# Reciprocal roots of two neighbouring units in one GpSimd chain, and a rank of its own for every step

## The chip, the cores and the metric

The kernel runs on one core of one Trainium2 chip. The metric is the time on the device in microseconds: 1473.11 us, the median of 3 runs (1471.62 to 1473.71).

## The reference

Agent attention followed by a feed-forward layer with a SoLU and a layer norm, in four batches of 12608 tokens, with 128 channels, 49 agents and 1024 hidden units:

```python
def sm(a, b):                      # softmax over the last axis
    s = scale * (a @ b.transpose(0, 2, 1))
    e = np.exp(s - s.max(-1, keepdims=True))
    return e / (e.sum(-1, keepdims=True) + 1e-09)
agent_v = sm(agents, k) @ v
x = (sm(q, agents) @ agent_v).reshape(B * N, 128)
h = x @ w_in
sm_ = softmax(h)
solu = h * sm_
ln = (solu - mean(solu)) / np.sqrt(var(solu) + 1e-06) * g_ln
out = ln @ w_out
```

q, k and agents are drawn with a standard deviation of 0.8; w_in and w_out arrive as 64-bit floats and are converted on the chip.

## The kernel before, in words

The tokens are worked on in tiles of 128, 99 to a batch, 396 in all. A batch has two stages. In the first (`phase_a`), the keys and values are read in chunks of 1024 (12 and a rest of 320), scored against the agents (line 523), exponentiated, transposed (line 556) and multiplied with the values (line 577); the result, folded with w_in, is a pair of matrices, `mh` and `ml`. The first stage of batch b+1 is run among the tiles of batch b. In the second, `phase_b` forms the softmax of eight tiles of queries against the agents, and then each tile goes through these steps: scores `h` on TensorE (`c_h`, line 867, four matmuls), their maximum on VectorE (`c_max`, line 871), the exponential on ScalarE with its sum S (`c_exp`, line 881), the product u on VectorE (`c_u`, line 886), and the sum of squares Q on ScalarE (`c_sq`, line 892).

Then come the output products. Two tiles are a pair, two pairs are a unit of four tiles. Pairs are of kinds Z and Y in turn (`PAT = "ZYZY"`), so a Z unit and a Y unit are interleaved and end one pair apart; the last four pairs are Z. A Z unit transposes u on TensorE (line 899), evacuates it on ScalarE into `uT` (line 952), splits it on GpSimd into a high and a low part (lines 961 and 965) and multiplies them with the two parts of w_out (`c_w`, line 982); the product stands in a PSUM bank until `c_fin` (line 1053) on VectorE multiplies it by the roots `rB`. A Y unit transposes u in blocks on VectorE (`c_tb`, line 906), moves the blocks with 16 DMAs from SP's queue (`c_mv`, line 916), multiplies in full float (`c_wy`, line 922) and is scaled by its roots `yp` on ScalarE or VectorE (`c_fy`, line 930 or 932).

The roots are formed for each unit once its four tiles' S and Q are there (`c_rstd`): eight instructions on GpSimd over four columns (lines 993 to 1014; the fourth is a power of -1/2, line 1002, then follows one step of Newton's rule), a transposition `yr` on VectorE (line 1018), a DMA `dr` into DRAM (line 1022) and one back: spread over all partitions as `rB` for a Z unit (line 1026), as one column a tile, `yp`, for a Y unit (line 1044). The last unit takes another way, over TensorE.

The order of the work is written out by a planner in the kernel (`Plan`). Each step is an op with engines, a planned cost, a due time, and the ops that it waits for. The planner walks through time; for each engine it looks at the ops that could start within a short margin and takes the one with the smallest due time. The due times are the tile's number plus an offset by kind of step (`DH`, `DMX`, ...), some sixty constants. There are two banks of two for the scores and four single PSUM banks that the planner hands out to all other products. What it writes down is the order of each engine's instructions and of SP's queue; the waits on the chip follow from the data.

Of the kernel before, what the change touches and what calls it, by code (L numbers as in the profile page):

```python
# [16 lines left out]
PSUM = bass.MemoryType.PSUM  # L17

# [7 lines left out]
class Plan:  # L26
# [158 lines left out]
def pair_kinds(n):  # L185

    kinds = ["Z" if i >= n - 4 else PAT[i % len(PAT)] for i in range(n)]
    if kinds.count("Y") % 2:
        kinds[max(i for i in range(n) if kinds[i] == "Y")] = "Z"
# [11 lines left out]
def kernel(  # L201
# [18 lines left out]
    GT = 4  # L220
# [7 lines left out]
    CPR = 514.07  # L228
# [17 lines left out]
    BD0 = 1.55  # L246
    BD1 = 43.9
    BD2 = 323.81
    BD3 = -61.67
    BD4 = 161.19  # L250
    BD5 = -3.79
    DH = -7.09
    DMX = 12.27
    DEX = -557.66
    DU_ = -32.48
    DSQ = 235.38
    DT = -63.56
    DCP = -36.06
    DEV = 13.48
    DLD = -39.18  # L260
    DSP = 47.88
    DW = 22.04
    DR = -5.79
    DF_ = 10.97
    DRB = -20.24
    OUTD = -9.57
    OUTC = -74.75
    VA = 3
    VA1 = 12
    QA = 41.77  # L270
    WA = 314.18
    VLAG = 98.2
    PTB = 4
    SHY = -80.96
    DHR = -337.25
    DHL = -85.23
    DMXR = -12.05
    DMXL = -147.69
    DEXR = 107.68
    DEXL = -205.84  # L280
    DUR = -296.62
    DUL = -37.59
    DSQR = -186.3
    DSQL = -311.69
    DTR = 73.98
    DTL = -151.89
    DEVR = -27.37
    DEVL = -372.85
    DLDR = -297.34
    DLDL = 160.86  # L290
    DSPR = -202.86
    DSPL = -50.83
    DWR = 84.18
    DWL = 1.45
    RBL = -442.9
    ASP = 1.09
    MZ = 2.36
    DTB = -3.22
    DMV = -110.03
    DMS = -223.53  # L300
    MVC = 1
    DWY = 28.21
    DWS = 5.02
    YC = 8
    DFY = 54.59
    DTBR = -12.62
    DTBL = -3.65
    ASTART = -9.62
# [133 lines left out]
    nhalf = const.tile([P, GT], F32, name="nhalf")  # L442
# [35 lines left out]
    def phase_a(b, due, gate):  # L478
# [188 lines left out]
        def kop(c):  # L667
            if c < NC and c not in K:
                old = M1.get(c - 1) if not head else None
                K[c] = op("S", st(kload, c), (0.45, sz(c), 0), -199 + 0.2 * c if head else at(c * 2.55 - 3), gate + [old])  # L670

        def vop(c):
            old = M2.get(c - 1) if not head else M1[3] if 4 <= c < 8 else M1[7] if 8 <= c < NCK else None
            V[c] = op("S", st(vload, c), (0.45, sz(c), 0), -199 + 0.2 * c + VLAG if head else at(c * 2.55 - 2), gate + [old])
# [16 lines left out]
        for c in range(NC):  # L691
# [4 lines left out]
            if not head:  # L696
# [3 lines left out]
            EE[c] = op("A", st(p1_exp, c), 0.665 if c < NCK else 0.742, at(z + 0.5), [N1[c], TT.get(c - EKB)], free=M1[c])  # L700
            TT[c] = op("P", st(p2_t, c), 0.435 * fr(c), at(z + 1), [EE[c], M2.get(c - 2) if not head else None], take=True)
            ET[c] = (op("A", st(p2_et, c, "A"), 0.478 * fr(c), at(z + 1.2), [TT[c]], free=TT[c]) if head and c < HEADA else
                     op(ETE, st(p2_et, c), (0.478 * fr(c), 0.6 * fr(c)), at(z + 1.2), [TT[c]], free=TT[c]))
# [32 lines left out]
    BT, B0, B4, B5, BQ, pT_op, grp_h = {}, {}, {}, {}, {}, {}, {}  # L736
# [17 lines left out]
    def phase_b(k, dues, gate=()):  # L754
# [74 lines left out]
        d1 = op("D", b1, 0.047 + 0.0532 * nt, dues[1], [prev], shy=shy)  # L829
        d2 = op("D", b1s, 0.05 + 0.0532 * nt, dues[1] + 0.1, [d1] + [B4.get((k - 2, q)) for q in range(2)], free=first, shy=shy)  # L830
        a1 = op("A", b2, 0.098 + 0.0402 * nt, dues[2], [d2])
        d3 = op("D", b3, 0.05 + 0.0532 * nt, dues[3], [a1], shy=shy)
        d5 = op("D", b3r, 0.12, dues[3] + 0.2, [d3])
        for q in range(nq):
# [7 lines left out]
            B5[k, q] = op("P", lambda px, q=q: b5(q, px), 0.33 * sc, dues[5] + 2.5 * q, [B4[k, q]], take=True, shy=shy)  # L842
# [9 lines left out]
    order = {"Y": 0, "Z": 0}  # L852
# [20 lines left out]
    def c_exp(x):  # L873
        G, j = slot[x]
        if G not in st:
# [93 lines left out]
    def c_w(i, m0, m1, px=None):  # L969
        G = unit[i]  # L970
        h = units[G][1].index(i)
# [12 lines left out]
    def c_rstd(G):  # L984
        gp = nc.gpsimd
        r = {}

        def r0():
            for z in "txyz":
                r[z] = tiny.tile([P, GT], F32, tag=z, bufs=SB, name=f"{z}{G}")  # L990
            r["yt"] = ycol[G % 2]
            r["yc"] = r["yt"][:, :: SQB // GT]
            gp.tensor_scalar(out=r["t"], in0=st[G]["S"], scalar1=1e-9, scalar2=math.sqrt(1e-6 * DF), op0=ALU.add, op1=ALU.mult)
# [4 lines left out]
        def r2():  # L998
            gp.tensor_tensor(out=r["x"], in0=st[G]["Q"], in1=r["t"], op=ALU.add)

        def r3():
            gp.tensor_tensor(out=r["y"], in0=r["x"], in1=nhalf, op=ALU.pow)
# [13 lines left out]
        def r8():  # L1016
            r["yr"] = tiny.tile([P, SQB], F32, tag="yr", name=f"yr{G}")
# [6 lines left out]
        def sent(e):  # L1024
            rB = st[G]["rB"] = opool.tile([P, GT, GT, SQB], F32, tag="rB", bufs=3, name=f"rB{G}")
            port[e].dma_start(out=rB.rearrange("d a j p -> d (a j p)"),
                              in_=r["dr"].rearrange("j p -> (j p)").unsqueeze(0).to_broadcast([P, P * GT]))

        def d0():
            r["dg"] = epool.tile([P, GT, P], F32, tag="uT", bufs=UTB, name=f"dg{G}")  # L1030
# [7 lines left out]
        def d2():  # L1038
            rB = st[G]["rB"] = opool.tile([P, GT, GT, SQB], F32, tag="rB", bufs=3, name=f"rB{G}")
            nc.scalar.copy(out=rB.rearrange("d a j c -> d j a c"), in_=r.pop("px").rearrange("d (j a c) -> d j a c", a=GT, c=SQB))  # L1040

        def senty(e):
            yp = st[G]["yp"] = tiny.tile([P, GT], F32, tag="yp", name=f"yp{G}")
            port[e].dma_start(out=yp, in_=r["dr"].rearrange("j p -> (j p)").rearrange("(a p) -> p a", p=P))
# [5 lines left out]
    def c_fin(G, j0=0, j1=GT):  # L1050
        rB = obs[G] = st[G]["rB"]
        z = rB.rearrange("d a j c -> d j a c")[:, j0:j1]
# [34 lines left out]
    for q, cost in enumerate((1.23, 0.64, 0.35)):  # L1087
        os_ = op("G", F(sums, q), cost, OUTD, og + [os_])
    om = op("P", mean, 0.22, OUTD, [os_], take=True)
# [9 lines left out]
    TBT, MV, WY, FY, OO, YP, R2, CP = ({} for _ in range(8))  # L1099
    utl, pol = [], {}  # L1100
    nth, seen = {}, {"Y": [], "Z": []}
    for G, (kd, _) in enumerate(units):
        nth[G] = len(seen[kd])
        seen[kd].append(G)
    zpairs = [i for i in range(n // 2) if units[unit[i]][0] == "Z"]
    zix = {i: z for z, i in enumerate(zpairs)}

    def back(G, k):
        z = nth[G] - k
        return seen[units[G][0]][z] if z >= 0 else None  # L1110
    ku = 0
    for x in range(n):
# [3 lines left out]
        isY = kind[x] == "Y"  # L1116
# [9 lines left out]
        MX[x] = op("D", F(c_max, x), 1.13, at(x, DMX, DMXR, DMXL), [H[x, 0], H[x, 1]])  # L1126
# [151 lines left out]
```

## Time and profile before

| | before |
|---|---|
| median of 3 runs | 1473.11 us |
| span of the profiled execution (its own time) | 1472.9 us |
| TensorE matmuls busy | 1444.4 us (98%) |
| TensorE weight loads busy | 1279.7 us (87%) |
| VectorE busy | 1376.2 us (93%) |
| ScalarE busy | 1291.1 us (88%) |
| GpSimd busy | 1071.1 us (73%) |
| DMA | 221.90 MB, mean 151 GB/s |

In the rows below, PE is TensorE's matmuls and PEld its weight loads, DVE VectorE, ACT ScalarE, POOL GpSimd, SP or SPq the queue that issues the DMAs; L12 is line 12 of the kernel. Busy times are of one profiled execution. Matmuls are pipelined and their ends are modelled, so a busy TensorE is not TensorE at its peak. Idle time of an engine that is not the bottleneck costs nothing.

### The profile page before, as it was taken

Reading aid. Unit: us, or ns where it says so; the run is one execution under the profiler, and the core shown is the slowest. Engines: PE = TensorE matmul, PEld = TensorE weight load, DVE = VectorE, ACT = ScalarE, POOL = GpSimd, SP = SyncE. Lnnn points to the kernel's source line nnn. Section 1 sums busy time; section 2 is a strip of 40 time slices with the busy share of each in tenths; the row PEclk is TensorE's granted clock in tenths of the full one; section 3 lists DMA queues with packets and bytes.
Section 4 is the critical chain, followed back from the end, with each engine's and each line's share of the span. In section 5 each row is a group of like instructions: output and inputs, shape, how many; then the busy total and the mean of one; then the engine's idle time right before and its main releaser. Section 6 shows DMA issues by size and latency. Waiting matters only on the chain.

```text
span 1472.9 us, 33358 instructions
## 1 busy us (share of the span) xinstructions
PE 1444.4 (98%) x12033; PEld 1279.7 (87%) x12033; DVE 1376.2 (93%) x2024; ACT 1291.1 (88%) x2486; POOL 1071.1 (73%) x1521
## 2 busy tenths in 40 slices
PE   8889999999999999999999999999999999999998
PEld 4668889898888898899898798998999999999998
DVE  5899999999999999999989899999999999999985
ACT  5489999999898998899987898988989999999985
POOL 2485887777776777688677667787768887887854
PEclk9899999999999999999999999999999999999999
DMA  9356565565456756654746666566455455554541
GB/s 369 130 137 194 145 166 149 152 160 142 130 140 187 183 144 160 155 167 114 191 105 159 175 169 175 142 164 166 113 140 135 116 150 131 132 142 106 138 107 44
DMA packets 113253, 221.90 MB, mean 151 GB/s; under 512 B 47552, under 2 KB 50880, under 8 KB 113088
## 3 DMA queue, kind: packets, MB, share of 16 engines
q1 hardware_dynamic: 113088, 219.77, 55.7%
q8 instruction: 95, 1.56, 0.5%
q14 instruction: 70, 0.57, 0.1%
HBM read 92.87 MB, written 26.15 MB: 81 GB/s over the span
## 4 chain that ended last, share of the span: by engine, by line
PE 64%; DVE 15%; ACT 12%; issue 4%; DMA 3%; SPq 2%; POOL 0%; ACTq 0%; DVEq 0%; POOLq 0%
PE ph L867 16%; PE px L922 16%; PE px L982 13%; PE px L899 8%; DVE u L886 5%; ACT e L881 5%; DVE nm L871 4%; ACT uT L952 3%; ACT e L892 3%; PE px L523 3%; DVE tb L906 3%; PE px L577 3%; PE px L767 2%; SPq L916 2%; PE px L812 1%
## 5 line engine op out<-in xcount | busy, mean ns | idle before, releaser
L881 ACT ACTIVATE e<-ph,nm 128x1024 f32<-128x1024 f32 x396 | 443.3, 1123 | 88.1 <-DVE nm L871 84.4
L871 DVE TENSOR_REDUCE nm<-ph 128x1 f32<-128x1024 f32 x396 | 467.2, 1207 | 31.8 <-PE ph L867 29.9
L886 DVE SCALAR_TENSOR_TENSOR u<-ph,e 128x1024 f32<-128x1024 f32 x396 | 471.7, 1218 | 18.7 <-ACT e L881 15.1
L965 POOL TENSOR_TENSOR uL<-uT,uH 128x1024 fp32r<-128x1024 f32 (+1 forms) x198 | 471.3, 2380 | 12.2
L892 ACT ACTIVATE e<-u,su 128x1024 bf16<-128x1024 f32 x396 | 459.1, 1163 | 20.2 <-DVE u L886 19.6
L922 PE MATMUL px<-w,uY 128*128 128x128 f32 x3072 | 375.6, 276 | 0.0
L922 PEld LDWEIGHTS px<-w,uY 128*128 128x128 f32 x3072 | 359.9, 192 | 13.9 <-issue 8.4
L867 PE MATMUL ph<-mh,pT 128*128 128x512 f32 x792 | 335.4, 423 | 7.7 <-DVE u L886 7.3
L867 PE MATMUL ph<-ml,pT 128*128 128x512 f32 x792 | 312.8, 395 | 1.9 <-DVE ml L653 1.9
L961 POOL TENSOR_SCALAR uH<-uT 128x1024 fp32r<-128x1024 f32 (+1 forms) x198 | 207.8, 1049 | 87.0 <-ACT uT L952 87.0
L982 PE MATMUL px<-uH,wH 128*128 128x256 f32 x816 | 237.8, 291 | 0.4 <-ACT eT L567 0.4
L906 DVE STREAM_TRANSPOSE tb<-u 128x1024 f32<-128x1024 f32 x192 | 235.8, 1233 | 0.7
L982 PE MATMUL px<-uH,wL 128*128 128x256 f32 x816 | 228.4, 280 | 0.0
L982 PE MATMUL px<-uL,wH 128*128 128x256 f32 x816 | 228.0, 279 | 0.0
L952 ACT COPY uT<-px 128x512 f32<-128x512 f32 x394 | 213.7, 597 | 11.7 <-PE px L899 11.1
L899 PE MATMUL px<-ident,u 128*128 128x128 f32 x1632 | 218.1, 275 | 1.1 <-ACT uT L952 0.6
L899 PEld LDWEIGHTS px<-ident,u 128*128 128x128 f32 x1632 | 186.2, 142 | 15.8 <-ACT uT L952 3.8
L867 PEld LDWEIGHTS ph<-mh,pT 128*128 128x128 f32 x792 | 150.1, 190 | 39.5 <-DVE u L886 13.4
L867 PEld LDWEIGHTS ph<-ml,pT 128*128 128x128 f32 x792 | 150.7, 190 | 24.4 <-DVE ml L653 2.3
L982 PEld LDWEIGHTS px<-uH,wH 128*128 128x128 f32 x816 | 153.8, 188 | 15.6 <-issue 11.4
L982 PEld LDWEIGHTS px<-uL,wH 128*128 128x128 f32 x816 | 155.2, 190 | 3.7 <-issue 0.5
L982 PEld LDWEIGHTS px<-uH,wL 128*128 128x128 f32 x816 | 153.7, 188 | 0.0
(127 smaller groups left out, 1570.1 us busy)
## 6 DMA issues: line engine op xcount, KB each, us to landing
uY<-tb SPq DMA_DIRECT2D x768, 128.0 KB, 2.6
qt<-in_qT_dram SPq DMA_DIRECT2D x48, 512.0 KB, 4.2
kt<-in_kT_dram SPq DMA_DIRECT2D x36, 512.0 KB, 4.4
vt<-in_v_dram SPq DMA_DIRECT2D x36, 512.0 KB, 4.1
rB<-dr SPq DMA_DIRECT2D x50, 256.0 KB, 4.1
out_dram<-rB SPq DMA_DIRECT2D x50, 256.0 KB, 2.0
out_dram<-oy SPq DMA_DIRECT2D x48, 256.0 KB, 2.7
kh<-in_kT_dram SPq DMA_DIRECT2D x12, 512.0 KB, 8.7
```

The source lines that it names most:

```text
L867: nc.tensor.matmul(ph[:, sl], lhs, bmats[b]["mh" if m == 0 else "ml"][:, sl], start=(m == 0), stop=(m == 1))
L871: nc.vector.tensor_reduce(out=nms[x], in_=phs[x], op=ALU.max, axis=AX.X, negate=True)
L881: nc.scalar.activation(out=es[x], in_=phs[x], func=AF.Exp, bias=nms.pop(x), accum_out=st[G]["S"][:, j : j + 1])
L886: nc.vector.scalar_tensor_tensor(out=u, in0=phs[x], scalar=INV, in1=es[x], op0=ALU.mult, op1=ALU.mult, accum_out=su)
L892: nc.scalar.activation(out=sq, in_=u, func=AF.Square, bias=su, scale=-float(DF), accum_out=st[G]["Q"][:, j : j + 1])
L899: nc.tensor.transpose(pt[:, kf * P : (kf + 1) * P], us[x][0][:, k0 * P : (k0 + 1) * P], ident)
L906: nc.vector.transpose(to, us[x][0].rearrange("p (k r c) -> p k r c", r=GT, c=SQB))
L922: nc.tensor.matmul(st[G]["po"][:, a * P : (a + 1) * P], yb[G][1][:, a, kf].rearrange("p x c -> p (x c)"), w2[:, kf, :], start=(kf == 0), s ...
L952: nc.scalar.copy(out=rr[x][:, hf * 4 : hf * 4 + 4, :], in_=pt)
L961: nc.gpsimd.tensor_scalar(out=uH, in0=rr[x][:, k0:k1, :], scalar1=1.0, scalar2=0.0, op0=ALU.mult, op1=ALU.add)
L965: nc.gpsimd.tensor_tensor(out=uL, in0=rr[x][:, k0:k1, :], in1=uH.bitcast(F32), op=ALU.subtract)
L982: nc.tensor.matmul(po, wt[:, kf, :], ut[:, kf, :], start=(q == 0), stop=(q == WM - 1))
```

## The change

Neighbouring units, in the order in which they end, share one chain for their roots. `chains` lists them, `link` tells of each unit its chain and its place in it. S and Q are now tiles of eight columns for a chain, of which each unit uses four; the eight GpSimd instructions, the transposition and the DMA `dr` are done once for a chain, after the last tile of its last unit; `rB` and `yp` are read back for each unit as before.

Each op's due time is no longer worked out from the offsets but read from a table in the order in which the ops are made (`RANKS`, a compressed list of 16-bit numbers). The offsets stand in the code with other values, but the table overrides them. Margins of the planner are changed too, and many ops get an `after`, which fixes their order among their like without a wait on the chip. There are other smaller edits: a Y unit's first matmul waits for the scaled output of the Y unit before (`back(G, 1)`, it was `back(G, 2)`), the ring of S and Q holds four chains (it held six units), and there is a third kind of unit, X, with functions of its own, which the pattern does not use.

```diff
+RANKS = (
...
+        raw = zlib.decompress(base64.b85decode(RANKS))
+        self.ranks = [z / 40 - 100 for z in struct.unpack(f"<{len(raw) // 2}H", raw)]
+        self.made = 0
...
     def op(self, eng, fn, cost, due, deps=(), take=False, free=None, after=(), kind=1, shy=0.0):
         o = Op()
+        due = self.ranks[self.made]
+        self.made += 1
...
-    EP = 0.14
-    EA = 0.09
-    ED = 0.0
-    EG = 2.33
-    HLD = -3.7
-    STK = 1.57
+    EP = 0.15
+    EA = 0.1
+    ED = 0.1
+    EG = 1.0
+    HLD = -3.0
+    STK = 1.0
...
-    SB = 6
+    SB = 4
...
+    ends = sorted(range(len(units)), key=lambda G: units[G][1][-1])
+    chains, link = [], {}
+    for z, G in enumerate(ends):
+        if chains and len(chains[-1]) == 1 and units[G][1][-1] - units[chains[-1][0]][1][-1] <= 2 and z < len(ends) - 1:
+            chains[-1].append(G)
+        else:
+            chains.append([G])
+        link[G] = (len(chains) - 1, len(chains[-1]) - 1)
...
+            st["c", c] = [tiny.tile([P, 2 * GT], F32, tag=z, bufs=SB, name=f"{z}{c}") for z in "SQ"]
...
-            st[G] = {
-                "S": tiny.tile([P, GT], F32, tag="S", bufs=SB, name=f"S{G}"),
-                "Q": tiny.tile([P, GT], F32, tag="Q", bufs=SB, name=f"Q{G}"),
-            }
+            st[G] = {z: t[:, u * GT : (u + 1) * GT] for z, t in zip("SQ", st["c", c])}
...
-    def c_rstd(G):
+    def c_rstd(c):
         gp = nc.gpsimd
+        m = len(chains[c]) * GT
+        step = SQB // (2 * GT)
...
-            dr = r["dr"] = dpool.tile([GT * GT, SQB], F32, tag="dr", bufs=4, name=f"dr{G}")
-            port[e].dma_start(out=dr, in_=r["yr"][:: SQB // GT, :])
+            dr = r["dr"] = dpool.tile([GT, 2, GT * SQB], F32, tag="dr", bufs=4, name=f"dr{c}")
+            port[e].dma_start(out=dr.rearrange("a u (j q) -> (a u j) q", q=SQB), in_=r["yr"][::step, :])
...
-        MX[x] = op("D", F(c_max, x), 1.13, at(x, DMX, DMXR, DMXL), [H[x, 0], H[x, 1]])
+        MX[x] = op("D", F(c_max, x), 1.13, at(x, DMX, DMXR, DMXL), [H[x, 0], H[x, 1]], after=[MX.get(x - 1)])
...
-                    prev = op("P", f, 0.224 * YC, x + DWY + DWS * q / (GT * NF // YC), (mv if q == 0 else []) + [prev, FY.get(back(G, 2)) if q == 0 else None] + wready, take=q == 0, kind=4)
+                    prev = op("P", f, 0.224 * YC, x + DWY + DWS * q / (GT * NF // YC), (mv if q == 0 else []) + [prev, FY.get(back(G, 1)) if q == 0 else None] + wready, take=q == 0, kind=4)
...
-        if j == GT - 1:
-            first, rest, turn, send, sent, (d0, d1, d2), senty = c_rstd(G)
-            mine = [2 * z + q for z in units[G][1] for q in range(2)]
+        ci, cu = link[G]
+        if j == GT - 1 and cu == len(chains[ci]) - 1:
+            first, rest, turn, send, sent, (d0, d1, d2), senty = c_rstd(ci)
+            mine = [2 * z + q for z_ in chains[ci] for z in units[z_][1] for q in range(2)]
```

## Rows read from the trace of the kernel before

**Rows 1.** The page's first part: busy us, share of the span, instructions.
```profile
PE 1444.4 (98%) x12033; PEld 1279.7 (87%) x12033; DVE 1376.2 (93%) x2024; ACT 1291.1 (88%) x2486; POOL 1071.1 (73%) x1521
```

**Rows 2.** Busy time by stretch: stretch, length, each engine, granted clock, DMA.
```profile
0.00:120.00 120.00, 102.12 (x835) 70.67 (x836) 98.99 (x177) 77.12 (x162) 61.53 (x92) 0.93 0.64 216
120.00:1200.00 1080.00, 1073.79 (x9010) 959.04 (x9008) 1028.70 (x1502) 971.99 (x1864) 805.18 (x1139) 1.00 0.58 152
1200.00:1400.00 200.00, 199.98 (x1667) 186.31 (x1666) 196.63 (x273) 191.12 (x368) 166.57 (x235) 1.00 0.52 131
1400.00:1473.00 73.00, 68.50 (x528) 63.63 (x526) 51.88 (x75) 50.91 (x96) 37.78 (x57) 1.00 0.27 74
```

**Rows 3.** The same, of line 867 alone: matmuls, then weight loads.
```profile
120.00:1080.00 960.00, 299.01 (x1080) 187.72 (x1080) 1.00 0.59 155
1200.00:1320.00 120.00, 38.73 (x151) 26.35 (x149) 1.00 0.54 136
```

**Rows 4.** Chain that ended last, first batch's keys: start, us, what.
```profile
17.96 1.01 PE px L523 x4
...
26.02 0.44 PE px L556 x4
...
41.44 1.02 PE px L577 x16
```

**Rows 5.** Groups by line: count, busy us, mean ns, idle before.
```profile
L1002 POOL TENSOR_TENSOR y<-x,nhalf 128x4 f32<-128x4 f32 x99 | 100.2, 1012 | 7.7
...
L1014 POOL TENSOR_TENSOR ycol<-y,z 128x4 f32<-128x4 f32 x99 | 20.3, 205 | 8.1
...
L1018 DVE STREAM_TRANSPOSE yr<-ycol 128x32 f32<-128x32 f32 x98 | 19.3, 197 | 4.0 <-POOL ycol L1014 3.8
L993 POOL TENSOR_SCALAR t<-S 128x4 f32<-128x4 f32 x99 | 19.3, 195 | 56.1 <-ACT e L881 51.0
```

**Rows 6.** Timeline of GpSimd, 1196 to 1231 us: start, length, what.
```profile
1197.10 0.19 POOL L993 TENSOR_SCALAR t<-S 128x4 f32<-128x4 f32 x1
...
1206.29 0.19 POOL L993 TENSOR_SCALAR t<-S 128x4 f32<-128x4 f32 x1
...
1209.07 0.20 POOL L1014 TENSOR_TENSOR ycol<-y,z 128x4 f32<-128x4 f32 x1
```

**Rows 7.** Waits of the whole span: us in total, times, longest.
```profile
PEld px L899 <- ACT uT L952: 3.8, 15, 0.8
...
PEld px L812 <- POOL ycol L1014: 1.6, 2, 0.8
```

**Rows 8.** Timeline of SP's queue, 1204 to 1231 us.
```profile
1205.18 0.38 SPq L1026 DMA_DIRECT2D rB<-dr  x1
1207.42 10.59 SPq L916 DMA_DIRECT2D uY<-tb  x16
1218.11 0.54 SPq L1022 DMA_DIRECT2D dr<-yr  x1
```

**Rows 9.** Timeline of VectorE, 1204 to 1231 us.
```profile
1210.02 0.19 DVE L1018 STREAM_TRANSPOSE yr<-ycol 128x32 f32<-128x32 f32 x1
...
1222.43 0.67 DVE L1053 TENSOR_TENSOR rB<-px,rB 128x512 f32<-128x512 f32 x1
```

**Rows 10.** DMA issues: count, KB each, median us to landing.
```profile
rB<-dr SPq DMA_DIRECT2D x50, 256.0 KB, 4.1
...
dr<-yr SPq DMA_DIRECT2D x98, 2.0 KB, 1.8
```

**Rows 11.** Timelines of ScalarE and of TensorE, 1204 to 1231 us.
```profile
1207.10 1.13 ACT L930 ACTIVATE oy<-px,yp 128x128 f32<-128x128 f32 x4
...
1210.25 1.95 PE L922 MATMUL px<-w,uY 128*128 128x128 f32 x16
```

**Rows 12.** Chain that ended last, 0 to 125 us: start, us, what.
```profile
47.98 1.42 DVE ca_out L368
...
54.95 1.60 POOL w L368
...
56.57 1.51 DVE w L368
...
60.39 2.26 DVE nm L871 x2
```

More of the change, by code (lines that the diff above doesn't have):

```diff
@@ L1 @@
+import base64
 import math
+import struct
+import zlib
 from contextlib import ExitStack
@@ L187, in pair_kinds @@
     kinds = ["Z" if i >= n - 4 else PAT[i % len(PAT)] for i in range(n)]
-    if kinds.count("Y") % 2:
-        kinds[max(i for i in range(n) if kinds[i] == "Y")] = "Z"
+    for k in "YX":
+        if kinds.count(k) % 2:
+            kinds[max(i for i in range(n) if kinds[i] == k)] = "Z"
     units, open_ = [], {}
@@ L244 @@
     WC = 12
[L246 to L257, printed above, removed]
[L258 to L267 removed]
+    BD0 = -19.07
+    BD1 = 170.81
+    BD2 = -212.77
+    BD3 = 221.79
+    BD4 = -125.09
+    BD5 = 89.47
+    DH = -1001.84
+    DMX = 537.76
+    DEX = -742.92
+    DU_ = -73.14
+    DSQ = 242.69
+    DT = -560.39
+    DCP = -36.06
+    DEV = -708.6
+    DLD = 138.29
+    DSP = 144.95
+    DW = 41.63
+    DR = -236.61
+    DF_ = 250.94
+    DRB = 136.25
+    OUTD = 224.28
+    OUTC = 373.93
     VA = 3
     VA1 = 12
[L270 to L272 removed]
+    QA = 346.14
+    WA = -635.12
+    VLAG = 213.44
     PTB = 4
     SHY = -80.96
[L275 to L288, printed above, removed]
[L289 to L300 removed]
+    DHR = 270.45
+    DHL = -42.04
+    DMXR = -1193.55
+    DMXL = 333.78
+    DEXR = 361.3
+    DEXL = 36.12
+    DUR = 35.14
+    DUL = -402.67
+    DSQR = 322.29
+    DSQL = 377.68
+    DTR = -72.36
+    DTL = -80.02
+    DEVR = -59.2
+    DEVL = 324.83
+    DLDR = -297.34
+    DLDL = 69.77
+    DSPR = -732.04
+    DSPL = 136.84
+    DWR = -382.0
+    DWL = -6.98
+    RBL = -442.9
+    ASP = 1.072
+    MZ = 1.612
+    DTB = 266.92
+    DMV = 56.0
+    DMS = -370.6
     MVC = 1
[L302 to L303 removed]
+    DWY = -89.82
+    DWS = 936.93
     YC = 8
[L305 to L308, printed above, removed]
+    DFY = -17.85
+    DTBR = -297.4
+    DTBL = -15.69
+    XPOS = 3
+    XGAP = 2
+    DXP = 3.0
+    DXS = 3.0
+    DXW = 6.0
+    DFX = 8.0
+    ASTART = 3.06
     AEND = -155.17
@@ L1098 @@
     H, MX, EX, U, SQ, T, EV, LD, SH, SP, W, FIN, RB, TN = ({} for _ in range(14))
[L1099 to L1110, printed above, removed]
+    TBT, MV, WY, FY, OO, YP, R2, UYD, SD = ({} for _ in range(9))
@@ new lines, with back @@
+    utl, pol, LY, LZ = [], {}, {}, {}
+    sets = ("Y", "Z", "X", "YX", "ZX")
+    nth, seen = {}, {z: [] for z in sets}
+    for G in ends:
+        kd = units[G][0]
+        for z in sets:
+            if kd in z:
+                nth[G, z] = len(seen[z])
+                seen[z].append(G)
+    def back(G, k, z=None):
+        z = z or units[G][0]
+        m = nth[G, z] - k
+        return seen[z][m] if m >= 0 else None
+    gseq = sorted([(2.0 * i, i) for i in range(n // 2) if units[unit[i]][0] == "Z"]
+                  + [(min(2.0 * units[G][1][-1] + 1.5 + XPOS + XGAP * h, n - 4.4 + 0.1 * h), (G, h)) for G in seen["X"] for h in range(2)], key=lambda z: z[0])
@@ new lines, with spare @@
+    gix = {k: z for z, (_, k) in enumerate(gseq)}
+    AL, R0, UA, last_t = {}, {}, [os0], None
+    closed, opened, room = [], [], {}
+    for _, k in gseq:
+        G, h = k if isinstance(k, tuple) else (unit[k], units[unit[k]][1].index(k))
+        if h == 0:
+            assert len(opened) <= 1
+            room[G] = closed[: len(closed) - (1 - len(opened))][-1:]
+            opened.append(G)
+        else:
+            opened.remove(G)
+            closed.append(G)
+    def spare(G):
+        return [FIN.get(z) for z in room[G]]
@@ new lines, in gprev, with split, unit_x @@
+    def gprev(k, m):
+        z = gix[k] - m
+        return gseq[z][1] if z >= 0 else None
+    def split(k, src, d, f, g, k0=0, k1=NF):
+        a = op("G", f, 0.2 + 0.115 * (k1 - k0), d, src + [W.get(gprev(k, ZB))], after=AL.get(gprev(k, 1), []))
+        AL.setdefault(k, []).append(a)
+        return a, op("G", g, 0.2 + 0.268 * (k1 - k0), d + 0.02, [a])
+    late = []
+    def unit_x(pos, k):
+        G, h = k
+        for q in (2 * h, 2 * h + 1):
+            SH[G, q], SP[G, q] = split(k, MV[G][q * GT : q * GT + GT], pos + DXP + DXS * q / GT, F(c_xh, G, q), F(c_xl, G, q))
+        prev = W.get(gprev(k, 1))
+        for m0 in range(0, WM, WC):
+            m1 = min(m0 + WC, WM)
+            lead = m0 == 0 and h == 0
+            f = (lambda px, m1=m1: c_w(k, 0, m1, px)) if lead else F(c_w, k, m0, m1)
+            prev = op("P", f, 0.1172 * (m1 - m0), pos + DXW + 2.0 * m0 / WM,
+                      [SH[G, 2 * h], SP[G, 2 * h], SH[G, 2 * h + 1], SP[G, 2 * h + 1]] + wready + [prev] + (spare(G) if lead else []),
+                      take=lead, kind=3)
+            if lead:
+                pol[G] = [prev]
+        W[k] = prev
+        UYD[G] = UYD.get(G, []) + [SP[G, 2 * h], SP[G, 2 * h + 1]]
+        if h:
+            FIN[G] = op("D", F(c_fin, G), 0.62, pos + DFX, [prev, RB[G]], free=pol[G][-1])
+            OO[G] = op("S", F(c_out, G), (0.48, 0.26, 0), pos + DFX, [FIN[G]])
@@ L1115 @@
         i = x // 2
-        isY = kind[x] == "Y"
+        kd = kind[x]
+        while late and late[0][0] < x:
+            unit_x(*late.pop(0))
         if t % UB == 0:
```

300 lines of the change are left out of this document (232 added, 68 removed).

## The prediction

> **What bounds the kernel now.** I read the page's busy shares first, then busy time by stretch, then waits, chain and timeline. TensorE is busy for 1444.4 of 1472.9 us, VectorE for 93%, ScalarE for 88%, GpSimd for 73% [rows 1]. A matmul's busy time is modelled, so the shares alone do not say that TensorE is the limit. The stretches do [rows 2]: from 1200 to 1400 us, in the last batch, where no keys of a next batch are left to work on, TensorE is busy for 199.98 of 200 us and VectorE for 196.63. In the 1080 us before, TensorE idles 1080 - 1073.79 = 6.2 us. In the first 120 us it idles 17.9, in the last 73 us 4.5. That is 28.6 us in all.
>
> Does the modelled time hide more in the middle? The score matmuls of line 867 are four to a tile, so a row's matmuls divided by four count tiles [rows 3]: 1080 / 4 = 270 tiles in 960 us are 3.56 us a tile, 151 / 4 = 37.75 in 120 us are 3.18. The 0.38 between them is 102 us over 270 tiles. In that stretch the matmuls of the next batch's keys are added, 1.01 + 0.44 + 1.02 = 2.47 us a chunk [rows 4], some 12.3 chunks in each of three batches, 91 us. So about 11 us stay for everything that a better order could win there, the 6.2 us of idle among them. The middle is at the limit of TensorE to about 1%.
>
> **The change, part by part.** All durations are of the profiled execution, whose span is 1472.9 us; the median of the runs is 1473.11, so 0.2 us is added at the end.
>
> *GpSimd's chain.* There are 99 units and 99 chains of eight instructions. Seven take 0.195 to 0.205 us, the power 1.012 [rows 5]: 2.42 us busy, and in one piece 1209.07 + 0.20 - 1206.29 = 3.0 us from start to end [rows 6]. The units end in the order Z, Y, Z, Y, one pair of tiles apart. The rule of the diff makes 48 chains of a Z and a Y unit, one of two Z units near the end, and leaves the last Z unit alone: 50. So 49 x 8 = 392 instructions go, 49 x 2.42 = 118.6 us. What eight columns cost is not in the trace: if the time goes with the instruction nothing is added, if all of it goes with the columns, the whole 118.6 us is. The row nearest is the chain's own: with equal columns the power takes 0.81 us longer than the others, so I let that part alone double: 49 x 0.81 = 40 us. GpSimd then has 1071 - 119 + 40 = 992 us, 67%. All of it lies beside TensorE, which hardly waits for it: of its waits for GpSimd's chain 1.6 us are the largest [rows 7]. Value 0, bounds -2 to +2.
>
> *VectorE and SP.* 49 transposes of 0.197 us go [rows 5], 9.7 us of 1376, and 49 sends of 0.5 us on SP [rows 8]. VectorE's part counts only where TensorE waits for it. In the last batch, where both are full, 49 / 4 = 12 transposes are 2.4 us. Value -1, bounds -2.4 to 0. SP's is worth 0: its queue is not what ends last, apart from the next point.
>
> *The Z unit's roots come later.* This is the wait that the change adds. Z's chain begins at 1197.10, Y's at 1206.29, 9.2 us behind [rows 6], and the merged one can do no better than Y's. Now Z's broadcast (rB) is issued at 1205.18, lands 4.1 us later at 1209.3, and the product that needs it (line 1053) starts at 1222.43 [rows 8, 9]: 13.1 us in hand. Y's transposed roots stand at 1210.02, but their send goes at 1218.11, behind sixteen moves of uY that hold SP for 10.59 us from 1207.42 [rows 8]. If the merged send stays behind them, rB goes 1.8 us after it [rows 10] and lands at about 1218.1 + 1.8 + 4.1 = 1224.0, 1.6 us after the product wants it, and a PSUM bank is held as much longer. If the send is ranked ahead of most of the moves, it is issued near 1210.5, rB lands near 1216.4, and nothing is late. Behind rB in SP's queue stand the query load and the outputs, which have room; the moves of uY are what a send ahead of them delays, by 0.5 us. Bounds 0 and +12 us (the price is worked out under the rivals). I take +0.5: one period in the list is not the rule for all, and the send has an order of its own to be placed in.
>
> *One Y accumulator.* The first matmul of a Y unit now waits for the previous Y unit's scaled output instead of the one before that. Before, that output ends at 1207.10 + 1.13 = 1208.2 and the next lead begins at 1210.25 [rows 11], so the new wait is met already. Value 0; if an order wants them overlapped it costs that order a bank, no more than the 0.25 us below.
>
> *The ring of four chains* covers 3 x 8 tiles back where six units covered 5 x 4: not tighter, 0. The unit kind X and its functions are not reached: the pattern is still ZYZY.
>
> *The order.* Every step now takes its due time from a table, so each engine's queue can change. What can be won is bounded by the idle time above. The head: 17.9 us idle. There VectorE is busy for 98.99 of 120 us and the clock is 0.93 [rows 2]; the chain runs through the conversion of w_out on GpSimd and VectorE from 47.98 to 58.08 (56.57 + 1.51), ahead of the first row maxima at 60.39 [rows 12]. Those 10 us can partly go behind the first tiles, but VectorE must do the work somewhere before the first output product. I take -4, bounds -10 to +5. The middle: -3 of 11, bounds -11 to +10, the upper from an order that keeps as many gaps again as now. The last 73 us: -1.5 of 4.5, bounds -4.5 to +3.
>
> Sum: 0 - 1 + 0.5 + 0 - 4 - 3 - 1.5 = -9.0 us. 1472.9 - 9.0 + 0.2 = 1464.1, forecast **1464 us**, its own range 1456 to 1470.
>
> **Rivals.** (a) *TensorE's limit leaves nothing.* The gaps move and do not close. For it: 199.98 of 200 us, and a middle at 1%. Against: 28.6 us of idle are there. Time 1471 to 1476, say 1473.
>
> (b) *The late broadcast, slower.* The send stays behind the moves of uY, rB lands after the product wants it, and the bank comes free late in each of 48 pairs. The price of a late bank is that of TensorE waiting for an evacuation now, 3.8 us in 15 waits, 0.25 us [rows 7]: 48 x 0.25 = 12 us, 1485; with the won head and tail 1480. For it: 1.6 us short by the rows. Against: 13.1 us in hand where the send is not blocked. It decides from the point where rB lands after the last output matmul of its Z unit.
>
> (c) *More than the idle time.* The modelled matmul time hides pauses, and weight loads tell of them: loads fill 186.31 / 200 = 93% of the stretch from 1200 on, but (959.04 + 186.31 + 63.63) / 1353 = 1208.98 / 1353 = 89% of all after 120 us [rows 2]. At 93% throughout, 1208.98 / 0.932 = 1298 us follow the first 120: 1418 at the limit, about 1445 at half of it. Against: the key matmuls move 512 columns for one load, so their stretch has a smaller load share with no pause, and the pace above leaves 11 us, not 50. This is the rule of the Trainium skill, Perfetto Trace Analysis, "Identifying the Most-Contended Engine", that a matmul's busy time is no measure of the distance to the limit and the busy share of weight loads is; by it TensorE would have 13% left where the matmul row says 2%. By that rule the time would be nearer 1445; the trace's pace by tile does not agree that so much is left.
>
> (d) *The change does not relieve GpSimd:* the columns double all the cost. Then the time is that of the forecast, as nothing waits there.
>
> **How the numbers follow.** What a measurement of this kernel tells from no change is about 0.2%, 3 us. Forecast and (d) 0.48; a larger gain out of the same idle time, to 1448, 0.14; (c) 0.04; (a) 0.15; (b), or an order that opens new gaps by a few us, 0.19. Faster: 0.48 + 0.14 + 0.04 = 0.66; same 0.15; slower 0.19. The range takes in the larger gain and most of (b): 1448 to 1480 leaves out (c), the last part of the larger gain and the upper part of (b).
>
> **What would show it.** Right: GpSimd at 67 to 70% with 400 chain instructions, the power at up to 1.8 us; 49 transposes to yr; TensorE's idle in the first 120 us down by 3 to 6 us and in the middle to about 3; the same 3.18 us a tile in the last batch. Wrong: a product at line 1053 that waits for rB dozens of times (b); a pace in the middle below 3.45 us a tile (c); equal idle times in all stretches (a). If the pace of the last batch itself moves by more than 0.05 us a tile, the claim that TensorE is at its limit there is wrong.

## The result and the profile after

| | before | after |
|---|---|---|
| median | 1473.41 us (4 runs, 1471.62 to 1474.53) | 1490.28 us (4 runs, 1487.84 to 1498.66) |
| span of the profiled execution | 1472.9 us | 1490.8 us |

The change makes the kernel slower by 1.3%: ratio 1.0128, interval 1.0098 to 1.0158. The forecast was 1464 us, its range ended at 1480. The times of the kernel after also lie further apart than those of before.

The page's first part, as in [rows 1]. GpSimd has 86.5 us less to do and no engine has 18 us more; the time was not lost in work.

```profile
PE 1445.6 (97%) x12020; PEld 1275.2 (86%) x12020; DVE 1382.9 (93%) x2001; ACT 1278.4 (86%) x2415; POOL 984.6 (66%) x1129
```

Busy time by stretch, with the columns of [rows 2]. TensorE idles 13.4 us in the first 120 (17.9 before), then 22.2 (6.2), 5.5 (0.02) and 4.3 (4.5): 45.4 against 28.6 in all, which is the 17.9 us by which the span grew, but for 1.1. The head got better; the middle and the last batch got worse.

```profile
0.00:120.00 120.00, 106.61 (x931) 78.04 (x933) 100.63 (x183) 81.68 (x171) 64.66 (x88) 0.97 0.63 211
120.00:1200.00 1080.00, 1057.82 (x8800) 939.78 (x8796) 1019.02 (x1462) 943.13 (x1774) 718.75 (x814) 0.99 0.57 151
1200.00:1400.00 200.00, 194.48 (x1626) 177.54 (x1626) 189.15 (x255) 179.67 (x334) 147.41 (x164) 1.00 0.52 128
1400.00:1491.00 91.00, 86.72 (x670) 79.80 (x669) 74.14 (x104) 73.92 (x140) 53.72 (x65) 0.99 0.33 86
```

The score matmuls alone (line 1020, which was 867), as in [rows 3]. 1052 / 4 = 263 tiles in 960 us are 3.65 us a tile (3.56 before). For the last batch a stretch of 280 us serves better than the 120 of [rows 3], since the tiles do not come evenly: in slices of 40 us before had 42 to 53 of these matmuls. 342 / 4 = 85.5 tiles are 3.27 us a tile before (not the 3.18 of the short stretch), 328 / 4 = 82 are 3.41 after. First the two stretches of after, then the last batch of before.

```profile
120.00:1080.00 960.00, 287.73 (x1052) 184.11 (x1052) 0.99 0.58 154
1120.00:1400.00 280.00, 89.67 (x328) 57.21 (x328) 1.00 0.52 129
```

```profile
1120.00:1400.00 280.00, 88.94 (x342) 59.91 (x340) 1.00 0.52 131
```

Waits of the whole span (us in total, times, longest), first of after, then those rows of before that answer and did not stand above.

```profile
PEld ph L1020 <- DVE u L1039: 29.4, 57, 2.8
...
DVE rB L1226 <- DMA rB<-dr: 23.5, 22, 2.3
...
PE ph L1020 <- DVE u L1039: 10.4, 15, 2.3
...
DVE nm L1024 <- PE ph L1020: 8.3, 11, 1.7
```

```profile
DVE nm L871 <- PE ph L867: 29.9, 57, 2.0
...
PEld ph L867 <- DVE u L886: 13.4, 22, 2.4
...
PE ph L867 <- DVE u L886: 7.3, 6, 2.3
...
DVE rB L1053 <- DMA rB<-dr: 1.0, 1, 1.0
```

Two things are to be seen. VectorE now stands at line 1226 (the product `c_fin`, line 1053 before), 22 times, for the read-back of the roots; before, it did so once, for 1.0 us. And who waits for whom has turned round: before, VectorE waited 29.9 us for TensorE's scores, and TensorE for VectorE's u 13.4 with its weight loads and 7.3 with its matmuls; after it is 8.3 against 29.4 and 10.4. (A load and a matmul can stand for the same u, so the two are not added.)

One such wait, in the period round 1230 us. First GpSimd's timeline (start, length, what), then SP's queue, VectorE and TensorE.

```profile
1217.57 0.20 POOL L1160 TENSOR_SCALAR t<-S 128x8 f32<-128x8 f32 x1
...
1219.85 0.20 POOL L1166 TENSOR_TENSOR x<-Q,t 128x8 f32<-128x8 f32 x1 [1.79 <-ACT e L1045]
...
1220.48 1.65 POOL L1169 TENSOR_TENSOR y<-x,nhalf 128x8 f32<-128x8 f32 x1
1222.09 1.05 POOL L1126 TENSOR_SCALAR uH<-uT 128x1024 fp32r<-128x1024 f32 x1
1223.23 2.38 POOL L1130 TENSOR_TENSOR uL<-uT,uH 128x1024 fp32r<-128x1024 f32 x1
...
1227.41 0.21 POOL L1181 TENSOR_TENSOR ycol<-y,z 128x8 f32<-128x8 f32 x1
```

```profile
1220.80 8.89 SPq L1069 DMA_DIRECT2D uY<-tb  x14
1229.79 0.54 SPq L1189 DMA_DIRECT2D dr<-yr  x1
1230.37 1.51 SPq L1069 DMA_DIRECT2D uY<-tb  x2
1232.18 0.36 SPq L1194 DMA_DIRECT2D rB<-dr  x1
```

```profile
1229.03 0.19 DVE L1185 STREAM_TRANSPOSE yr<-ycol 128x32 f32<-128x32 f32 x1
...
1236.07 0.69 DVE L1226 TENSOR_TENSOR rB<-px,rB 128x512 f32<-128x512 f32 x1 [0.98 <-DMA rB<-dr]
1236.68 1.22 DVE L1039 SCALAR_TENSOR_TENSOR u<-ph,e 128x1024 f32<-128x1024 f32 x1
```

```profile
1236.91 0.36 PE L1146 MATMUL px<-uH,wH 128*128 128x256 f32 x1 [0.40 <-DVE rB L1226]
```

The chain takes 1227.41 + 0.21 - 1217.57 = 10.1 us from start to end: GpSimd waits 1.8 us in it for the last square, splits a u for 3.4 us between its steps and does 1.5 us of other work. The transposition follows 1.4 us later, the send 0.6 after its end, the read-back 2.4 after the send, and the product starts 3.9 us after the read-back's issue. It was 13.1 us behind its roots in the period of [rows 8, 9]; here it has stood for 0.98 us. Behind it in VectorE's queue stand the next two u, and TensorE's next output matmul waits 0.40 us for the product itself.

Two single periods can mislead, so here are all of them, read one by one from the two traces. The chain, 3.0 us in [rows 6] and 10.1 here, takes 5.2 us in the median of the 99 before (3.0 to 13.1) and 7.1 in the median of the 50 after (3.0 to 13.2). For the 44 Z units from the third on, counted from the end of a unit's last square and in medians, its chain is done after 2.7 us before and 12.8 after: 6.9 of these pass until the last square of the Y unit, and 5.6 more until the chain's end. The read-back is issued after 9.7 us before and 20.1 after, while the product starts after 27.3 and 25.8. So the read-back landed 11.9 us ahead of the product before, in the median of all 50, and 0.1 after; 28 of the 50 products of after start within 0.3 us of it. Waiting for the Y unit used up most of the margin, a later end of the chain and a product put 1.5 us earlier the rest.

First and last u on VectorE (ns min/median/max, then first and last start), before and after. From the first to the last there are 1387.7 us before and 1412.7 after. So the span splits: up to the first u 57.6 - 63.0 = -5.4, between them +25.0, after the last 20.5 - 22.2 = -1.7; together +17.9 = 1490.8 - 1472.9.

```profile
L886 DVE SCALAR_TENSOR_TENSOR u<-ph,e x396: 1184/1219/1226, 63.0 to 1450.7; 128x1024 f32<-128x1024 f32 x198
```

```profile
L1039 DVE SCALAR_TENSOR_TENSOR u<-ph,e x396: 1171/1220/1226, 57.6 to 1470.3; 128x1024 f32<-128x1024 f32 x198
```

### The profile page after: what moved, and what is told of

It reads as the page before. It is cut to its first block, busy times and chain, and to the rows that moved or that the text cites. A ratio compares the mean times of both kernels' runs of the same rounds, so it can differ in the third digit from the quotient of the medians.

```text
span 1490.8 us, 32588 instructions
## 1 busy us (share of the span) xinstructions
PE 1445.6 (97%) x12020; PEld 1275.2 (86%) x12020; DVE 1382.9 (93%) x2001; ACT 1278.4 (86%) x2415; POOL 984.6 (66%) x1129
## 4 chain that ended last, share of the span: by engine, by line
PE 47%; DVE 21%; DMA 12%; SPq 9%; ACT 6%; issue 3%; POOL 2%; DVEq 0%; ACTq 0%; POOLq 0%
PE px L1075 13%; PE ph L1020 12%; PE px L1146 9%; SPq L1069 8%; DVE u L1039 7%; PE px L1052 6%; DMA rB<-dr 6%; DVE nm L1024 6%; DVE tb L1059 4%; ACT e L1034 3%; PE px L719 2%; DMA uY<-tb 2%; PE px L911 2%; PE px L665 1%; ACT e L1045 1%
## 5 line engine op out<-in xcount | busy, mean ns | idle before, releaser
L1130 POOL TENSOR_TENSOR uL<-uT,uH 128x1024 fp32r<-128x1024 f32 (+1 forms) x198 | 470.6, 2378 | 13.2
L1020 PE MATMUL ph<-mh,pT 128*128 128x512 f32 x792 | 336.0, 424 | 10.8 <-DVE u L1039 10.4
L1117 ACT COPY uT<-px 128x512 f32<-128x512 f32 x394 | 220.0, 588 | 16.5 <-PE px L1052 15.0
L1052 PE MATMUL px<-ident,u 128*128 128x128 f32 x1632 | 226.8, 276 | 4.1 <-DVE rB L1226 3.2
L1020 PEld LDWEIGHTS ph<-mh,pT 128*128 128x128 f32 x792 | 149.9, 189 | 55.4 <-DVE u L1039 29.4
L1020 PEld LDWEIGHTS ph<-ml,pT 128*128 128x128 f32 x792 | 150.3, 190 | 22.2 <-issue 0.5
## 6 DMA issues: line engine op xcount, KB each, us to landing
kh<-in_kT_dram SPq DMA_DIRECT2D x12, 512.0 KB, 10.1
```

The costliest lines, as they stand in the source:

```text
L1020: nc.tensor.matmul(ph[:, sl], lhs, bmats[b]["mh" if m == 0 else "ml"][:, sl], start=(m == 0), stop=(m == 1))
L1052: nc.tensor.transpose(pt[:, kf * P : (kf + 1) * P], us[x][0][:, k0 * P : (k0 + 1) * P], ident)
L1117: nc.scalar.copy(out=rr[x][:, hf * 4 : hf * 4 + 4, :], in_=pt)
L1130: nc.gpsimd.tensor_tensor(out=uL, in0=rr[x][:, k0:k1, :], in1=uH.bitcast(F32), op=ALU.subtract)
```

## The experiments

The theory: the roots of a Z unit now come from Y's later chain, and the product waits for them in VectorE's queue, with u and the row maxima of the next tiles behind it. Against it stood: the new order by itself costs the time, whatever the roots do; the power over eight columns makes the chain late; the read-back in four pieces for each partition (it was one) is slow. Ratios are to the kernel before, run beside it on the same chip. Only two of the twelve times fell inside a range that was stated (the old order without the wait, and the four pieces); the new order without the wait and its control, 1467 and 1475 us, missed theirs by about 1 us.

**A chain of its own for each Z unit, in the new order** (an edit of after).

```diff
+            if pair:
+                own_chain(chains[ci][0])
+                first, rest, turn, send, _, _, senty1 = c_one(chains[ci][1], 0)
```

> The changed kernel's order on TensorE, ScalarE and VectorE to the instruction, but each Z unit has a chain, a transposition, a send and a read-back of its own again, put into the queues as soon as its squares are there; Y's chain has four columns. Theory L (the loss is the late broadcast that the merging brings): line 1053's like waits for rB a few times at most (23.5 us in 22 waits before), and the time falls from 1490 to 1470-1476. Theory O (the loss is in the new order itself, with or without the merging): the waits for rB go and the time stays at 1486-1492.

1496.39 us, ratio 1.0160 (1.0146 to 1.0174). The time is above both ranges. The wait at the product is gone, but another stands in its place. VectorE's waits:

```profile
DVE yro L1254 <- POOL ycol L1250: 27.8, 21, 2.5
```

A transposition has a fixed place in VectorE's queue, and with 48 chains more GpSimd comes late for it; the next run shows for which. This run doesn't tell the theories apart. What it shows is that 27.8 us of another wait on VectorE cost about as much.

**Z's transposition 5 us later** (an edit of that kernel).

```diff
-                    m["t"] = s + 3.1
+                    m["t"] = s + 8.0
```

> As the run with a chain for each Z unit of its own in the changed kernel's order, but the Z unit's transposition stands 5 us later in VectorE's queue, since there it waited 27.8 us for GpSimd in place of the 23.5 us for rB. Theory L: now neither wait is there, 1468-1477. Theory O: 1485-1495.

1507.34 us, 1.0234 (1.0221 to 1.0247). The wait did not go away; the tag yro stands for Y's transposition also, and it is that one, at its old place, that GpSimd is late for: behind each of the seven waits between 410 and 620 us the roots are read back as `yp`, in this run and in the one above. VectorE's waits for roots grew by 4.4 us here and the time by 10.9, so these waits are not all that the time goes by. Putting the chains back without a new table is no clean test.

```profile
DVE yro L1254 <- POOL ycol L1250: 27.3, 23, 2.5
...
DVE rB L1293 <- DMA rB<-dro: 4.9, 3, 3.3
```

**Merged chains in the old order** (an edit of before: TensorE, VectorE and ScalarE in before's order without Z's transpositions, 48 chains over eight columns at Y's place).

```diff
+            if len(chains[ci]) == 2 and ci not in EXCL:
+                if cu == 0:
+                    first, rest, turn, send = (nop, nop), ..., nop, nop
+                    sent = lambda e, ci=ci: late_rb(ci, e)
+                else:
+                    first, rest, turn, send2, sent2, _, senty2 = c_two(ci)
```

> The kernel before, with its order on TensorE, ScalarE and VectorE to the instruction, and with one chain of eight columns for each of the 48 pairs of a Z and a Y unit, at the place of Y's chain; 48 transposes and sends less. Theory L: the product waits for rB in many of the 48 pairs, 1480-1490. Theory O: the merging costs nothing by itself, 1471-1476.

1518.07 us, 1.0309 (1.0292 to 1.0327). The merging alone, without the new order, costs 45 us, far above either range. VectorE's waits, then one period on SP's queue and on VectorE:

```profile
DVE rB L1139 <- DMA rB<-dr: 49.7, 24, 6.7
```

```profile
1231.20 10.66 SPq L930 DMA_DIRECT2D uY<-tb  x16
1241.96 0.55 SPq L1103 DMA_DIRECT2D dr<-yr  x1
1244.00 0.38 SPq L1108 DMA_DIRECT2D rB<-dr  x1
```

```profile
1247.33 0.69 DVE L1139 TENSOR_TENSOR rB<-px,rB 128x512 f32<-128x512 f32 x1 [1.04 <-DMA rB<-dr]
```

In this period it is, row for row, what the prediction described of a send that stays behind the sixteen moves, and the product stands for 1.04 us here, where 1.6 were worked out. The mechanism is shown; so is that its price is not 0.25 us a pair, as 45 us over 48 pairs are 0.9.

**The same with the product reading something else** (an edit of the kernel just shown; the Z units' roots are left out of the product, which has an output tile of its own, and rB has one buffer instead of three).

```diff
-        rB = obs[G] = st[G]["rB"]
+            obs[G] = opool.tile([P, GT, GT, SQB], F32, tag="oz", name=f"oz{G}")
-        ..., in1=z, op=ALU.mult)
+        ..., in1=w_, op=ALU.mult)
```

> The kernel before in its order with merged chains (1518 us), and the product of a Z unit reads w_in in place of rB (its roots are left out). If all that the merging costs in the old order is the late broadcast: 1470-1477. If the shorter GpSimd queue or the sends cost something beside it: 1485 or more.

Here `w_` is a part of win_sb, which is ready long before. 1471.26 us, 0.9991 (0.9982 to 1.0000). 46.8 us come back by taking away a wait of 49.7 (44.1 between the spans of the two profiled executions); VectorE's first wait is then again that for the scores, and all that merging costs in the old order is the late broadcast.

```profile
DVE nm L885 <- PE ph L881: 28.7, 54, 1.6
```

**The kernel after with the product reading something else** (the same edit, of after; the Z units' roots are left out).

> The changed kernel with every queue in the same order; the product of a Z unit reads a part of w_in that stands in SBUF since the start and not rB, so it waits for TensorE alone (the roots of the Z units are left out; rB is still sent and read back, by nobody used). Theory L (the loss is VectorE's wait for rB): 23.5 us of waits go and the time falls from 1490 to 1468-1476. Theory O (the new order loses elsewhere): 1483-1490, at most the 4 us that the kernel without the power gained.

1467.16 us, 0.9953 (0.9939 to 0.9966). 1490.28 - 1467.16 = 23.1 us for a wait of 23.5. The two runs were not made side by side; the intervals of their ratios allow 19 to 32 us, and the spans of the two profiled executions differ by 25.3. Two of the first waits of VectorE, the score matmuls by stretch (line 1020) and the first and last u follow. No wait for rB is left; 1072 / 4 = 268 tiles in 960 us and 342 / 4 = 85.5 in 280 us are 3.58 and 3.27 us a tile; and from first to last u there are 1387.8 us, as before the change.

```profile
DVE u L1039 <- ACT e L1034: 19.4, 71, 1.8
...
DVE nm L1024 <- PE ph L1020: 11.0, 15, 2.9
```

```profile
120.00:1080.00 960.00, 291.40 (x1072) 188.53 (x1072) 0.99 0.59 156
1120.00:1400.00 280.00, 92.13 (x342) 59.89 (x342) 1.00 0.53 131
```

```profile
L1039 DVE SCALAR_TENSOR_TENSOR u<-ph,e x396: 1171/1219/1227, 57.2 to 1445.0; 128x1024 f32<-128x1024 f32 x198
```

**The control: before with the same edit** (the Z units' roots are left out).

> The kernel before in its own order; the product of a Z unit reads w_in in place of rB (its roots are left out). Theory L: there is no wait for rB to take away in the old order (1.0 us once): 1471.5-1474. Rival: the in-place product with a tile that a DMA has just written costs VectorE something by itself, 1465-1470, and the gain of the run that read w_in in the new order is partly that.

1474.91 us, 1.0013 (1.0003 to 1.0022). Reading another tile gains nothing by itself, so the 46.8 and 23.1 us are those of the wait. What this shows is that the loss of the kernel after is the late rB; it does not by itself show why rB is late, for which there are the periods and medians above.

**The read-back in four pieces, alone** (an edit of before: `dr` laid out as in after, one unit to a chain).

```diff
-            dr = r["dr"] = dpool.tile([GT * GT, SQB], F32, tag="dr", bufs=4, name=f"dr{G}")
+            dr = r["dr"] = dpool.tile([GT, 2, GT * SQB], F32, tag="dr", bufs=4, name=f"dr{c}")
```

> The kernel before in its own order; only the scratch tensor of the roots has the layout of the changed kernel, so that a Z unit's read-back takes four pieces of 512 bytes a partition in place of one of 2 KB. If the pieces make the landing later: 4.3 to 4.6 us in place of 4.1 and, with 13 us in hand, the same time, 1472-1474. If they load the DMA queues beside it: 1476 or more.

1472.79 us, 1.0007 (0.9997 to 1.0017). The read-back lands in 4.3 us instead of 4.1 [rows 10], and with 13 us in hand that costs nothing. DMA issues:

```profile
rB<-dr SPq DMA_DIRECT2D x50, 256.0 KB, 4.3
```

**After without the power** (a product in its place; the roots are left out).

```diff
-            gp.tensor_tensor(out=r["y"], in0=r["x"], in1=nhalf[:, :m], op=ALU.pow)
+            gp.tensor_tensor(out=r["y"], in0=r["x"], in1=nhalf[:, :m], op=ALU.mult)
```

> The changed kernel with every queue in the same order; the power of -1/2 on GpSimd, 1.64 us over eight columns, is replaced by a product of 0.2 us, so the roots are left out and rB can land some 1.4 us earlier. Theory L: most of the 22 waits for rB, 1.07 us in the mean, go; VectorE gets back some 18 us and the time falls to 1474-1482. Theory O: VectorE's wait goes and the time stays at 1487-1492.

1485.84 us, 1.0086 (1.0073 to 1.0100). By the medians that is 4 us less than after, but the intervals touch, and the spans of the two profiled executions are 1489.7 and 1490.8. The wait did not get smaller:

```profile
DVE rB L1226 <- DMA rB<-dr: 29.8, 22, 2.8
```

The roots stand earlier on GpSimd (5.9 us from the chain's start to its end in the median, 7.1 in after), but the transposition and the send keep their places in VectorE's and SP's queues: the transposition now starts 1.7 us after the chain's end, 0.4 in after. So the dear power is not the cause. The theory had it that an earlier chain would bring rB earlier, and that was wrong too.

**The chain's steps first** (an edit of after: chain, transposition, send and read-backs get a rank ahead of all others, and the planner orders all anew).

```diff
-        due = self.ranks[self.made]
+        due = self.ranks[self.made] - (5000 if rush else 0)
```

> The changed kernel, but the merged chain's steps, its transposition, its send and its two read-backs go before every other step that their engine could take; the planner works the rest out anew around that. Theory L: rB lands 3 to 4 us earlier, hardly any wait for it, 1474-1480. Theory O: 1486-1495, whatever the waits for rB do.

1622.71 us, 1.1014 (1.0993 to 1.1035). VectorE's waits:

```profile
DVE nm L1024 <- PE ph L1020: 64.3, 63, 5.2
...
DVE rB L1226 <- DMA rB<-dr: 27.1, 12, 4.4
```

**The planner told what the chain costs** (an edit of after: 1.64 us for the power, 1 us more for the read-back; the same table).

```diff
-                    RB[G] = op("SA", F(sent, u), (0.5, 0.3, 0), ...)
+                    RB[G] = op("SA", F(sent, u), (0.5, 0.3, 1.0), ...)
```

> The changed kernel, but the planner reckons with 1.64 us for the power over eight columns in place of 1.02 and with 1 us more for the landing of rB (4.05 in place of 3.05; the trace has 4.4), so it places the product later; the table is the same. Theory L: fewer than 8 waits for rB, 1472-1480. Theory O: the order is another one and loses as much or more, 1485-1500.

1606.67 us, 1.0904 (1.0885 to 1.0922), again with the scores as VectorE's first wait (63.1 us in 68 times, where the order of after without the wait for rB has 11.0).

Both runs say nothing of the roots: the wait for rB is still there in both (27.1 us, and 26.9 in 16 times), and a loss of 130 to 150 us lies over it. With other ranks for a few steps, or with other planned times under the same ranks, the planner's list falls apart.

**The bank copied, the product put on GpSimd** (an edit of after: for 47 units VectorE only copies the bank, and GpSimd multiplies the copy by rB later).

```diff
+            nc.vector.tensor_copy(out=oz..., in_=st[G]["po", 0]...)
+                    nc.gpsimd.tensor_tensor(out=rB, in0=oz, in1=rB, op=ALU.mult)
```

> The changed kernel with TensorE's and ScalarE's queues in the same order. At the product's place VectorE only copies a Z unit's PSUM bank into SBUF, which waits for TensorE alone; the product with rB is done by GpSimd some 4 us of the plan later (47 of 51 Z units, each some 1.3 us on an engine that is busy for 66%), and the output goes out after it. Theory L: VectorE does not wait for rB any more, as in the run that read w_in in its place (1467): 1465-1471, faster than the kernel before. Rival: GpSimd waits for rB in its place, the splits of u behind it come late, 1474-1485.

1486.81 us, 1.0098 (1.0079 to 1.0117). The wait for rB is gone from VectorE, and one for the chain has come; GpSimd has more to do here:

```profile
DVE yr L1188 <- POOL ycol L1184: 23.4, 22, 7.9
```

**The same with transposition and read-back later** (the transposition of a merged chain 4 us later, send, read-backs and product behind it).

```diff
+            m["t"] = TN[ci].start + 4.0
```

> As the run with the product on GpSimd, where VectorE's wait went over from rB to the chain (yr waited 23.4 us for ycol in 22 waits), but the transposition of the roots stands 4 us of the plan later in VectorE's queue and the send, the read-backs and GpSimd's product behind it; TensorE's and ScalarE's queues are in the changed kernel's order. Theory L, put wider (the time follows what VectorE waits for the roots, at either of its two places): neither wait is there, 1464-1471, faster than the kernel before. Rival: GpSimd's added products themselves cost the time, by late splits of u: 1480-1487 again, with VectorE's waits gone.

1494.57 us, 1.0162 (1.0144 to 1.0179). The wait at the transposition is halved, and GpSimd now stands at its products:

```profile
DVE yr L1188 <- POOL ycol L1184: 11.8, 6, 4.3
...
POOL rB L1233 <- DMA rB<-dr: 7.7, 3, 5.9
```

VectorE also waits longer for the scores and for ScalarE than in the run before (16.4 and 24.3 us, 6.7 and 18.5 there); what costs the time in this run is not settled.

No version that computes everything was faster than the kernel before. Whether an order with merged chains can do without the wait stays open: it would take a new table of ranks.

## Why the prediction was wrong, by its own steps

*GpSimd's chain, 0:* right as to GpSimd's load. 49 transposes, 50 chains, GpSimd at 66% (just under the 67 to 70 forecast), the power at 1.63 us where "up to 1.8" stood. The page's groups, as in [rows 5]:

```profile
L1169 POOL TENSOR_TENSOR y<-x,nhalf 128x8 f32<-128x8 f32 (+1 forms) x50 | 81.5, 1630 | 3.3
...
L1185 DVE STREAM_TRANSPOSE yr<-ycol 128x32 f32<-128x32 f32 x49 | 9.9, 203 | 3.0 <-POOL ycol L1181 2.6
...
L1085 DVE TENSOR_TENSOR oy<-px,yp 128x512 f32<-128x512 f32 x33 | 22.3, 674 | 2.7 <-PE px L1075 2.7
```

*VectorE, -1:* the transposes went (19.3 to 9.9 us), but the new order puts more evacuations on VectorE, of oy 33 instead of 18 (22.3 us against 12.3), so its busy time rose by 6.7 us. With the wait away, VectorE is as busy (1381.4 us) and the time from first to last u is that of before, so no gain of this term shows.

*"The Z unit's roots come later", +0.5 with bounds 0 and +12:* this is the step that failed. It measured about +23 (19 to 32 by the intervals), and with it the time left the range. It was wrong in two ways.

First, whether rB is late. The prediction took it that a send ranked ahead of the moves would make nothing late. In the period shown the send does go at once, 0.57 us after the transposition ends, and two moves follow it; the margin was used up elsewhere. The 13.1 us in hand were one period's; the median was 11.9. Of these the wait for the Y unit took 6.9, where 9.2 were reckoned. The chain was taken as one piece of 3 us [rows 6], and its end came 5.6 us after the last square where a Z unit's had come 2.7 after its own. And the product moved: the new order put it 1.5 us earlier after the unit's last square, with a planned read-back of 3.05 us that took 4.4, and a planned power of 1.02 us that took 1.63. The product was left where it had been in the prediction, though it said that every queue can change.

Second, the price, which decides the size. The prediction said that "a PSUM bank is held as much longer" and priced that on TensorE, at 0.25 us a pair, from a wait for ScalarE's evacuation [rows 7]. TensorE's wait for the product is there: its matmuls waited 3.2 us at line 1052 in after, where they had never waited for it before. But the prediction did not name what is queued behind the product on its own engine. VectorE is busy for 93% of the span, u and the maxima stand behind the product, and TensorE's scores wait for u (29.4 us in its loads, 13.4 before). So a wait there passed to the end about one for one: 23.5 us of waits against 23.1 of time in the new order, 49.7 against 46.8 in the old. That is about 1 and 2 us for each of the 22 and 24 waits. It is a rough rule: without the power the wait was 29.8 us, and the time no longer. How much of the price goes over u and how much over the bank was not separated.

```profile
PE px L1052 <- DVE rB L1226: 3.2, 4, 1.0
```

*One Y accumulator, the ring, the unit kind X, 0:* not tried one by one; together with the order they cost nothing between the first and the last u once the wait is away (1387.8 against 1387.7 us).

*The order:* the head -5.4 (-4 forecast; TensorE's idle there fell by 4.5, "3 to 6") and the tail -1.7 (-1.5) were right as numbers. The head holds in all runs: the first u came at 60.9 to 63.0 us in the five kernels with the order of before, at 57.0 to 58.2 in the nine with the new table. But it did not come as forecast, so the number was in part luck: the conversion of w_out did not go behind the first tiles. VectorE still does all of it ahead of the first row maxima, and ends at 49.5 instead of 58.1 us [rows 12], as the conversions begin earlier (that of w_in at 8.8 us, 25.9 before).

```profile
48.50 0.98 DVE L510 SCALAR_TENSOR_TENSOR w<-wd_out,w 128x512 int32<-128x512 int32 x1
...
54.89 2.36 DVE L1024 TENSOR_REDUCE nm<-ph 128x1 f32<-128x1024 f32 x2 [1.54 <-PE ph L1020]
```

The middle's -3 was not there: 3.58 us a tile without the wait, 3.56 before. The 11 us from which it was taken came out of the short stretch of [rows 3]. With 3.27 us a tile in the last batch, 3.56 - 3.27 over 270 tiles are about 76 us, less than the 91 us of the keys' matmuls, so nothing was left to win by this reckoning. Without the Z term the forecast is 9.5 us under before; measured without the wait it was 1472.81 (before, on the same chip) - 1467.16 = 5.7 (5 to 9 by the interval).

*The rivals.* (b), the late broadcast, is what happened, at twice its price; its own sign, a product that waits for rB dozens of times, is in the waits (22). The other sign of being wrong came too: the pace of the last batch moved from 3.27 to 3.41 us a tile, more than 0.05, as TensorE idled there for 5.5 us of 200; with the wait away it is 3.27 again. (a) would have given 1471 to 1476 and falls, though without the wait the middle behaves as it says. (c) did not come: with the wait away the middle takes 3.58 us a tile, no less than before, and its sign was a pace below 3.45. The rule of the Trainium skill behind it (Perfetto Trace Analysis, "Identifying the Most-Contended Engine") judges what is left on TensorE by its useful work in the time (MFU), which was not worked out here, and by the busy share of weight loads. The loads were busy for 87%, and no run here shows such a gain: the fastest, with the wait away, is 0.5% under before. None was made to look for it either, so the rule is neither borne out nor refuted. (d) falls: GpSimd was relieved by 86.5 us, and nothing came of that.

## What to carry to other kernels

Where a change makes a result later, find the instruction that will wait for it, and price the wait by what stands behind it in that engine's queue; here, in an engine that is 93% busy, about as much time was lost as it waited. Read a margin over all periods and not off one, and do not carry it over to a new order: its steps stand elsewhere. Work out the margin again from the planned costs of every step of the chain, and compare these with the rows. Relieving an engine for which hardly anybody waits, here GpSimd by 86.5 us, gained nothing, so the later result was all that was left of the merging.

## What the runs showed of the hardware

The power on GpSimd got dearer with its columns: 1.01 us over four [rows 5], 1.63 over eight, while the other seven instructions of the chain stay at 0.20 to 0.21. So 50 powers of eight columns took 81.5 us where 99 of four took 100.2: most of what merging saved on GpSimd came from the seven cheap instructions. And a broadcast read-back of 256 KB, cut from one piece of 2 KB a partition into four of 512 bytes, landed in 4.3 to 4.4 us instead of 4.1 in the median of 50. In the order of before, which has room for it, that put 133,856 packets on the queue instead of 113,088 and changed the time by 0.07% (-0.03 to 0.17). DMA issues of the kernel after, as in [rows 10]:

```profile
rB<-dr SPq DMA_DIRECT2D x50, 256.0 KB, 4.4
```
